# Tile 3's eight chunks in seven half-size products, with weight sums partly on GpSimd

## The chip, the cores and the metric

The kernel runs on one core of one Trainium2 chip. The metric is the device time of one execution in microseconds (us). The core has five engines with instruction streams of their own: TensorE (PE; its weight loads are a row of their own, PEld), VectorE (DVE), ScalarE (ACT), GpSimd (POOL) and SyncE (SP, which here issues nearly all DMAs). Each engine works its stream in order and waits on semaphores for the others.

## The reference, cut to what matters

```python
for b in range(nb):                      # linear attention, decay lam per head, blocks of 64
    intra = einsum('bhic,bhjc->bhij', qb, kb) * Dmask
    intra = einsum('bhij,bhjd->bhid', intra, vb)
    inter = einsum('bhid,bhde->bhie', qb * lam_pow, kv_state)
    out[:, :, sl] = intra + inter
    kv_state = lam_block * kv_state + einsum('bhsd,bhse->bhde', kb * rev_pow, vb)
x = out.transpose(0, 2, 1, 3).reshape(3072, 512)
g = x @ w_gate                           # 512 x 1536
y = ((g / (1 + exp(-g))) * (x @ w_val)) @ w_out
```

Batch 4, 8 heads, 768 positions, head size 64; inputs and output are float32, the products run in bf16.

## The kernel before, in words

The 3072 rows of x are made in 12 attention **groups** of 256 rows (0 to 11); two groups make one **tile** of 512 rows, so there are six tiles, 0 to 5. Of a group g, in this order: `cast_scaled` (L287) casts k on ACT and q (times a decay) on DVE, into a `qk` buffer, and starts the DMA transpose; `v_scale` (L263) makes `v_s`; `upd_mm` (L406) multiplies k and v, ACT copies the result (`ups`, L446); `state` (L468) adds it up on POOL (`kvf`, L479; `kvn`, L459 and L461; `kvs`, L482; `kv`, L483); `scores` (L380) gives a mask product to DVE (L397); `inter`, `intra` (L507, L524) and `evac` (L538) put the group's rows into `xt`. `attend(g)` (L895) does inter of g, `upd_mm` and scores of g+1, intra and evac of g, then `state(g+1)`.

The FFN of a tile has 12 **chunks** fc of 128 hidden columns. A plain chunk (`ffn_fc`, L610) is four matmuls of 128x512 for the gate (L585), SiLU on ACT (L590), four for the value (L603) and a product on DVE (L607) that writes `h`. Chunks 0 to 5 are the first half of the hidden columns, 6 to 11 the second. The tiles 0 to 3 run as plain chunks, the tiles 4 and 5 as three `ffn_unit` calls each (L716). One unit does four chunks (2j, 2j+1, 6+2j, 7+2j) as a 2x2 block product in seven products instead of eight: each is 8 matmuls of 128x256 (L733), for gate and value together. It reads sums of weight blocks (`w_combo`, L681, in `ws`, one of four in place) and sums of x blocks (`x_combo`, L702, in `xs`), both on DVE; ACT copies two of the products (L767, L770), DVE adds (L775, L783) and multiplies (L763), and POOL does one of the four multiplications (L763). The output product is done in the same way from tile 1 on (`out_units`, L805, 84 matmuls a tile), with sums of `h` (`h_combo`, L655, L670, into `hs`) and of w_out (`wo_combo`, L644, L653, into `wt`) on DVE.

The eight PSUM banks go round in a ring (`bank`, L85): a chunk takes two of them, and the PE waits for a bank until ACT or DVE have read what was in it.

The order is written out by hand. `steps` (L1031) lists the chunks, `plan` (L1032) what is issued behind each of them, and the loop at L1184 walks through both. L1107 makes the first four chunks of tile 2 on its first group (`s2h`; the plan of the last of them, `s2`, holds the output of tile 0, attention of group 5 and the sums of `h` and w_out), and L1148 the rest of tile 2 (`sns[2]`: first those four chunks on the second group, then eight full ones) and tile 3 (`sns[3]`). The weight sums are put there by number (L1131): 110 and 112 are in tile 1, 206 and 210 in tile 2, 301 to 309 in tile 3. `trickle` holds the `h` sums, and `drip` issues a few of them behind each step.

```python
    WS = [(x, n, i, 0, 3) for x, n, i in ((110, 0, 0), (112, 0, 1), (206, 1, 0), (210, 1, 1), (301, 2, 0), (303, 2, 1))] + [(308, 3, 0, 0, 2), (309, 3, 1, 0, 2)]
...
        nc.vector.tensor_tensor(out=o, in0=i0, in1=i1, op=op)
```

Here the tuple is place, number of the sum, gate or value, and the columns; the second line is the sum itself (L696), 128x1536 in bf16.

Of the kernel before, what the change touches and what calls it, by code (L numbers as in the profile page):

```python
# [9 lines left out]
BF16 = mybir.dt.bfloat16  # L10
# [27 lines left out]
def _body(ctx, tc, nc, q, k, v, lam, moe_w_gate, moe_w_val, moe_w_out, out):  # L38
# [42 lines left out]
    last_bank = []  # L81

    fixed = []

    def bank():  # L85
# [4 lines left out]
        last_bank.insert(0, ring[0] % 8)  # L90
        b = banks[ring[0] % 8]
        primed[ring[0] % 8] = 0
        ring[0] += 1
        return b

# [186 lines left out]
        for put in held.pop(g, []):  # L282
            put()

    QP = ()

    def cast_scaled(g, eng=nc.vector):  # L287
        eng = nc.gpsimd if g in QP else eng
# [278 lines left out]
    def new_xt(t):  # L567
        st[("xt", t)] = xt_pool.tile([128, 2, MC, 2, BLK], BF16, name="xt", tag="xt")

    HALVED = ((2, 4), (2, 5))  # L570

    def pieces(t, fc, N, b0, b1):
        if (t, fc) in HALVED:
# [104 lines left out]
    ws = {}  # L678
    KH = MC // 2

    def w_combo(i, n, js=(0, 3)):  # L681


        w = (wg_sb, wv_sb)[i]
        if n < 2 and (i, n) not in ws:
            pool, tag = ((v_pool, "v"), (qk_pool, "qk"))[n]
            ws[i, n] = pool.tile([128, KH, FH * 128], BF16, name="ws", tag=tag)
        elif n == 2 and (0, n) not in ws:
            both = h_pool.tile([128, 2, KH, FH * 128], BF16, name="ws", tag="h")
# [10 lines left out]
    XS0 = 4  # L700

    def x_combo(t, n, g):  # L702


        xt = st[("xt", t)]
        g = slice(0, 2) if g is None else slice(g, g + 1)
        b11, b12 = xt[:, g, 0:KH, 0], xt[:, g, 0:KH, 1]
        b21, b22 = xt[:, g, KH:MC, 0], xt[:, g, KH:MC, 1]
        if t not in xs:
            pool, tag = (qkt_pool, "qkt") if t == XS0 else (raw_pool, "raw")  # L710
            xs[t] = pool.tile([128, 3, 2, KH, BLK], BF16, name="xs", tag=tag)
        x = [xs[t][:, m, g] for m in range(3)]
        o, i0, i1 = ((x[0], b12, b11), (x[1], b22, x[0]), (x[2], b21, x[1]), (b12, b22, b12))[n]
        nc.vector.tensor_tensor(out=o, in0=i0, in1=i1, op=ALU.subtract)

    def ffn_unit(t, j, bk, early=None, mid=None, dr=(0, 0, 2)):  # L716


        xt = st[("xt", t)]
# [10 lines left out]
        def product(i, o, lhs, rhs, start=False):  # L730
            for fi in range(2):
                for c in range(KH):
                    nc.tensor.matmul(o[:, fi * 256:fi * 256 + 256], lhs(i, c, 2 * j + fi), rhs(c),  # L733
                                     start=(start and fi == 0 and c == 0), stop=(c == KH - 1),
                                     skip_group_check=True)
# [410 lines left out]
    for t in range(2, 4):
        order = [c for j in range(FC // 4) for c in (2 * j, 2 * j + 1, FH + 2 * j, FH + 2 * j + 1)]
        sn = [step(t, fc, 2 if t == 2 and fc < NH else 0) for fc in (range(FC) if t == 2 else order)]  # L1148
        sns[t] = sn
        if t == 2:  # L1150
            at(sn[4], ahead, 6)
        for j, g in ((4 if t == 2 else 0, 2 * t + 3), (8 if t == 2 else 6, 2 * t + 4)):
            at(sn[j], cast_scaled, g)
            at(sn[j], load_group, g + 1)
            if g > 7:
                at(sn[1 + j], v_scale, g, nc.gpsimd, 0, H // 2)
                at(sn[(1 if t == 2 else 2) + j], v_scale, g, nc.gpsimd, H // 2, H)
        for i in range(2):
            at(sn[AT[t][i]], attend, 2 * t + 2 + i)
        if t == 2:  # L1160
            at(sn[4], out_units, 1, (0,), False, 2)
            at(sn[5], out_rest, 1, (0,), 2, 4)
            at(sn[6], out_rest, 1, (0,), 4, 7)
            at(sn[5], v_scale, 7, nc.vector)
            at(sn[8], out_units, 1, (1,), False, 2)
            at(sn[9], out_rest, 1, (1,), 2, 7)
            at(sn[9], h_combo, t, (0, 2))
        else:
            at(sn[7], h_combo, t, (0, 2))
        at(sn[11], h_combo, t, 2)  # L1170
    sn = sns[3]
    if C11 is not None:
        at(sn[C11], cast_scaled, 11)
# [4 lines left out]
    for x, n, i, j0, j1 in WS:
        at(sns[x // 100][x % 100], w_combo, i, n, (j0, j1))
    if not XM[0]:  # L1180
        for n in (0, 3, 1, 2):
            at(sn[XC], x_combo, 4, n, 0)

    for n, (t, fc, b0, b1) in enumerate(steps):  # L1184
        if t >= 1 and t + 1 < NG // 2 and ("xt", t + 1) not in st:
# [25 lines left out]
    xw = dict(x=x_soon(4, None if XM[0] else 1),
              c=[soon(cast_scaled, 11)] if C11 is None else [],
# [77 lines left out]
```

## Time and profile before

| what | us |
|---|---|
| median of 3 runs (216.4 to 217.43) | 216.51 |
| span of the profiled execution | 214.96 |
| PE busy (97% of the span) | 208.1 |
| DVE busy (69%) | 148.3 |
| ACT busy (61%) | 130.9 |
| POOL busy (43%) | 92.7 |
| granted TensorE clock | full throughout |
| tile 2's first four chunks on its second group | 81.47 to 85 |
| attention 6, attention 7 | from 97.4, from 108.8 |
| tile 3, twelve chunks | 111.7 to 135.4 |
| output of tile 2, 84 matmuls | 135.4 to 144.6 |

The profiled execution's own time outside its span is not recorded; the median lies 1.55 us above the span. Times in the views are counted from the start of the span. A row of the timeline gives start, duration, engine, line, operation, output and inputs, and in brackets how long the engine had stood idle and who ended that. A row of the chain gives start, duration, engine, tile, line and the number of instructions.

### The profile page before, as it was taken

The numbers are of one execution on the slowest core, as the hardware profiler recorded it, in microseconds if no ns is written. First come the engines' busy times: TensorE is split into PE (matmuls) and PEld (weight loads), VectorE is DVE, ScalarE is ACT, GpSimd is POOL, SyncE is SP. The second block draws the span as 40 slices with busy tenths as digits, with TensorE's granted clock in tenths as the row PEclk, the third lists the DMA queues.
The fourth block names the chain that finished last, engine by engine and source line by source line (L and its number), as shares of the span: only waits on it lengthen the run. The fifth ranks groups of instructions, "written<-read, shape, count | busy, mean of one in ns | idle before, by whom it ended". The sixth has DMA issues, their size and how long they took to land.

```text
span 215.0 us, 6856 instructions
## 1 busy us (share of the span) xinstructions
PE 208.1 (97%) x2797; PEld 153.3 (71%) x2801; DVE 148.3 (69%) x267; ACT 130.9 (61%) x280; POOL 92.7 (43%) x128
## 2 busy tenths in 40 slices
PE   8789999999999999999999999999999999999993
PEld 3467445887888548866754545888888888888883
DVE  1773447576677989874569878697988389961940
ACT  5878676756636153638369487774983676636522
POOL 6675755818399440595962153240750022200200
PEclk9999999999999999999999999999999999999999
DMA  6999999999999778899576859855000500005014
GB/s 188 345 354 381 376 336 296 285 226 223 309 387 174 185 212 208 244 214 263 122 198 143 217 121 257 207 121 201 5 3 5 195 0 3 0 0 198 0 52 146
DMA packets 82176, 39.76 MB, mean 185 GB/s; under 512 B 45410, under 2 KB 77794, under 8 KB 82146
## 3 DMA queue, kind: packets, MB, share of 16 engines
q1 hardware_dynamic: 80946, 38.74, 64.7%
q10 hardware_dynamic: 1200, 0.59, 0.9%
q8 instruction: 22, 0.36, 0.7%
q14 instruction: 8, 0.07, 0.1%
HBM read 28.31 MB, written 6.29 MB: 161 GB/s over the span
## 4 chain that ended last, share of the span: by engine, by line
PE 93%; DMA 2%; DVE 1%; SPq 1%; ACT 0%; issue 0%; DVEq 0%
PE bank L823 22%; PE bank L585 20%; PE bank L603 19%; PE bank L733 17%; PE bank L623 5%; PE bank L531 3%; DMA kraw<-in_k_dram 2%; PE bank L518 2%; PE bank L424 2%; PE bank L362 1%; DVE ssb L369 1%; SPq L115 1%; PE bank L392 1%; PE bank L322 1%; ACT qk L306 0%
## 5 line engine op out<-in xcount | busy, mean ns | idle before, releaser
L607 DVE TENSOR_TENSOR h<-sil,bank 128x256 bf16<-128x256 bf16 (+1 forms) x67 | 35.0, 533 | 29.9 <-PE bank L603 17.2
L585 PE MATMUL bank<-xt,wg_sb 128*128 128x256 bf16 (+1 forms) x276 | 52.8, 315 | 0.0
L603 PE MATMUL bank<-xt,wv_sb 128*128 128x256 bf16 (+1 forms) x276 | 52.5, 314 | 0.0
L590 ACT ACTIVATE sil<-bank 128x256 bf16<-128x256 f32 (+1 forms) x67 | 31.6, 481 | 21.8 <-PE bank L585 18.4
L603 PEld LDWEIGHTS <-wv_sb 128*128 128x128 bf16 x276 | 26.9, 98 | 14.8 <-POOL wv_sb L249 0.2
L585 PEld LDWEIGHTS <-wg_sb 128*128 128x128 bf16 x276 | 25.9, 98 | 13.6 <-issue 0.2
L266 POOL TENSOR_TENSOR v_s<-v,dec 128x512 bf16<-128x512 f32 (+1 forms) x18 | 23.0, 1295 | 24.3 <-DMA v<-in_v_dram 17.3
L763 POOL TENSOR_TENSOR h<-sil,es 128x512 bf16<-128x512 bf16 x6 | 7.0, 1165 | 47.4 <-ACT sil L760 47.4
L823 PEld LDWEIGHTS <-h 128*128 128x128 bf16 x240 | 23.3, 98 | 3.4 <-issue 0.3
L823 PE MATMUL bank<-wo_sb,h 128*128 128x256 bf16 x180 | 21.5, 273 | 0.0
L823 PEld LDWEIGHTS <-hs 128*128 128x128 bf16 x180 | 17.6, 98 | 2.7
L369 DVE TENSOR_TENSOR ssb<-bank,causal 128x512 bf16<-128x512 f32 x24 | 15.4, 684 | 1.8 <-PE bank L362 1.8
L479 POOL TENSOR_TENSOR kvf<-kvs,ups 128x256 f32<-128x256 f32 x8 | 6.5, 814 | 20.9 <-ACT ups L446 20.9
L733 PEld LDWEIGHTS <-ws 128*128 128x128 bf16 x144 | 13.8, 98 | 1.8
L823 PE MATMUL bank<-wt,hs 128*128 128x256 bf16 x120 | 15.0, 273 | 0.0
L775 DVE TENSOR_TENSOR bank<-bank,es 128x512 f32<-128x512 f32 x12 | 7.8, 694 | 9.6 <-PE bank L733 9.6
L479 POOL TENSOR_TENSOR kvf<-kvf,ups 128x256 f32<-128x256 f32 x16 | 13.0, 815 | 0.9
L760 ACT ACTIVATE sil<-bank 128x512 bf16<-128x512 f32 x18 | 10.5, 596 | 3.7 <-PE bank L733 3.7
L733 PE MATMUL bank<-xs,ws 128*128 128x256 bf16 x96 | 12.6, 273 | 0.0
L763 DVE TENSOR_TENSOR h<-sil,bank 128x512 bf16<-128x512 bf16 x18 | 11.8, 683 | 0.3 <-ACT sil L760 0.3
L623 PE MATMUL bank<-wo_sb,h 128*128 128x512 bf16 x45 | 10.7, 380 | 0.2
L733 PE MATMUL bank<-xt,wg_sb 128*128 128x256 bf16 x72 | 10.8, 273 | 0.0
(119 smaller groups left out, 360.3 us busy)
## 6 DMA issues: line engine op xcount, KB each, us to landing
out_dram<-osb SPq DMA_DIRECT2D x22, 256.0 KB, 2.6
v<-in_v_dram SPq DMA_DIRECT2D x18, 256.0 KB, 4.6
woraw<-in_moe_w_out_dram SPq DMA_DIRECT2D x6, 512.0 KB, 7.1
kraw<-in_k_dram SPq DMA_DIRECT2D x24, 128.0 KB, 3.4
qraw<-in_q_dram SPq DMA_DIRECT2D x24, 128.0 KB, 3.4
wraw<-in_moe_w_gate_dram SPq DMA_DIRECT2D x5, 512.0 KB, 6.9
wraw<-in_moe_w_val_dram SPq DMA_DIRECT2D x5, 512.0 KB, 7.0
kraw<-in_k_dram SPq DMA_DIRECT2D x4, 512.0 KB, 6.3
```

The costliest lines, as they stand in the source:

```text
L266: eng.tensor_tensor(out=st[("vs", g)][:, h0:h1], in0=st[("v", g)][:, h0:h1].rearrange("p h (s d) -> p h s d", s=2), in1=vfac(g, h0, h1), o ...
L369: nc.vector.tensor_tensor(out=ssb[:, h2, 2 * c:2 * c + 2].rearrange("p a s n -> p a (s n)"), in0=sp[(c, h2)].rearrange("p (a x) -> p a x", ...
L479: nc.gpsimd.tensor_tensor(out=o, in0=f, in1=u, op=ALU.add)
L585: nc.tensor.matmul(gp[:, n0:n1], wg_sb[:, mc, fs], xt[:, g0:g1, mc].rearrange("p g b n -> p g (b n)"), start=(mc == 0 and n0 == 0), stop=( ...
L590: nc.scalar.activation(sil[:, 0:N], gp[:, 0:N], AF.Silu)
L603: nc.tensor.matmul(vp[:, n0:n1], wv_sb[:, mc, fs], xt[:, g0:g1, mc].rearrange("p g b n -> p g (b n)"), start=(mc == 0 and n0 == 0), stop=( ...
L607: nc.vector.tensor_tensor(out=h_sb[:, fc % FH, b0:b1].rearrange("p b n -> p (b n)"), in0=sil[:, 0:N], in1=vp[:, 0:N], op=ALU.mult)
L623: nc.tensor.matmul(ps, st[("h", t, fc // FH)][:, fc % FH, b], wo_sb[:, fc, c0:c1], start=(fc == 0), stop=(fc == FC - 1))
L733: nc.tensor.matmul(o[:, fi * 256:fi * 256 + 256], lhs(i, c, 2 * j + fi), rhs(c), start=(start and fi == 0 and c == 0), stop=(c == KH - 1), ...
L760: nc.scalar.activation(sil[key], src, AF.Silu)
L763: eng.tensor_tensor(out=h_of(half, r), in0=v3(sil[half, r]), in1=v3(src), op=ALU.mult)
L823: nc.tensor.matmul(o, lhs(f), rhs(f), start=(start and f == 0), stop=(f == FH - 1), skip_group_check=True)
```

## The change

Tile 3's chunks 0 to 3 and 6 to 9 become two `ffn_unit` calls; chunks 4, 5, 10 and 11 stay plain, with attention 8 and 9 among them. For that the weight sums are wanted a tile earlier. Of the eight, four move to POOL: sum 0 of the gate behind `s2h`'s second chunk (place 113), sum 0 of the value and sum 1 of the gate behind `s2` (place 200), sum 1 of the value behind the seventh of tile 2's second list (206). The others stay on DVE, behind 206, 207 and 209. Since one sum overwrites w columns of chunks 6 to 9, tile 2 now does its chunks 6 to 11 first and 0 to 5 after them. Tile 3 gets its own x sums, behind attention 7, with a buffer for the fourth. The q cast of group 9 moves from DVE to POOL. The sums of tile 2's `h` all move behind its last chunk, attention 8's evacuation behind chunk 4, and a permutation of the banks fits the ring to the units.

```diff
-    QP = ()
+    QP = (9,)
...
-    HALVED = ((2, 4), (2, 5))
+    HALVED = ((2, 10), (2, 11))
...
-    def w_combo(i, n, js=(0, 3)):
+    def w_combo(i, n, js=(0, 3), eng=None):
...
-        nc.vector.tensor_tensor(out=o, in0=i0, in1=i1, op=op)
+        (eng or nc.vector).tensor_tensor(out=o, in0=i0, in1=i1, op=op)
...
-            pool, tag = (qkt_pool, "qkt") if t == XS0 else (raw_pool, "raw")
-            xs[t] = pool.tile([128, 3, 2, KH, BLK], BF16, name="xs", tag=tag)
+            pool, tag = (qkt_pool, "qkt") if t in XS0 else (raw_pool, "raw")
+            xs[t] = pool.tile([128, 4 if t == 3 else 3, 2, KH, BLK], BF16, name="xs", tag=tag)
...
-            product(i, E[i], wa(0, 1), xb(0, 1), True)
+            product(i, E[i], wa(0, 1), xsum(3) if t == 3 else xb(0, 1), True)
...
+        if add:
+            add()
...
-    s2h = [step(2, fc, 0, 2) for fc in range(NH)]
+    s2h = [step(2, fc, 0, 2) for fc in range(FH, FH + NH)]
...
-    WS = [(x, n, i, 0, 3) for x, n, i in ((110, 0, 0), (112, 0, 1), (206, 1, 0), (210, 1, 1), (301, 2, 0), (303, 2, 1))] + [(308, 3, 0, 0, 2), (309, 3, 1, 0, 2)]
+    PO, DV = nc.gpsimd, nc.vector
+    WS = [(113, 0, 0, 0, 3, PO), (200, 0, 1, 0, 3, PO), (200, 1, 0, 0, 3, PO), (206, 1, 1, 0, 3, PO),
+          (206, 2, 0, 0, 3, DV), (207, 2, 1, 0, 3, DV), (209, 3, 0, 0, 2, DV), (209, 3, 1, 0, 2, DV)]
...
+    sn = [step(2, fc, 2 if n < NH else 0) for n, fc in enumerate([*range(FH, FC), *range(FH)])]
...
+    at(sn[10], attend, 7)
+    at(sn[10], run_later, 1)
+    for n in (0, 3, 1, 2):
+        at(sn[10], x_combo, 3, n, None)
...
+    at(sn[11], h_combo, 2, (0, 2))
+    at(sn[11], h_combo, 2, 2)
...
+    for x, n, i, j0, j1, eng in WS:
+        at(s2 if x == 200 else sns[x // 100][x % 100], w_combo, i, n, (j0, j1), eng)
...
+    def cast9():
+        cast_scaled(9)
+        load_group(10)
+        for c in range(2):
+            v_scale(9, nc.gpsimd, c * H // 2, (c + 1) * H // 2)
+
+    ffn_unit(3, 0, (u0, u1, c0, c1, o0, o1), lambda: kv_flush(0, 2), dr=DU[0], add=cast9, hc=False)
+    ffn_unit(3, 1, (s0, s1, c0, c1, u0, u1), lambda: kv_flush(), dr=DU[1], hc=False)
+    h_combo(3, (0, 2))
+    perm[:] = [o0, o1, s0, s1, c0, c1, u0, u1]
+    ring[0] = 0
+    attend(8, soon=lambda: cast_scaled(10), fns=(None, None))
+    perm[:4] = [s0, s1, o0, o1]
+    load_group(11)
+    drip_2(DP[0])
+    plain(4)
+    evac(8)
...
+    attend(9)
+    run_later(1)
+    plain(FH + 5)
+    h_combo(3, 2)
```

More of the change, by code (lines that the diff above doesn't have):

```diff
@@ L83, in _body @@
     fixed = []
+    perm = list(range(8))
     def bank():
@@ L89, in bank @@
             return banks[fixed.pop(0)]
-        last_bank.insert(0, ring[0] % 8)
-        b = banks[ring[0] % 8]
-        primed[ring[0] % 8] = 0
+        last_bank.insert(0, perm[ring[0] % 8])
+        b = banks[perm[ring[0] % 8]]
+        primed[perm[ring[0] % 8]] = 0
         ring[0] += 1
@@ L631, in take @@
     def take(n, seeded, cols):
-        got = [(ring[0] + i) % 8 for i in range(n)]
+        got = [perm[(ring[0] + i) % 8] for i in range(n)]
         ring[0] += n
@@ L695, in w_combo @@
                          (s[2], a12, s[1], ALU.subtract), (a21, a11, a21, ALU.subtract))[n]
-        nc.vector.tensor_tensor(out=o, in0=i0, in1=i1, op=op)
+        (eng or nc.vector).tensor_tensor(out=o, in0=i0, in1=i1, op=op)
     xs = {}
     SY = 1
-    XS0 = 4
+    XS0 = (3, 4)
     def x_combo(t, n, g):
@@ L709, in x_combo, with ffn_unit @@
         if t not in xs:
-            pool, tag = (qkt_pool, "qkt") if t == XS0 else (raw_pool, "raw")
-            xs[t] = pool.tile([128, 3, 2, KH, BLK], BF16, name="xs", tag=tag)
-        x = [xs[t][:, m, g] for m in range(3)]
-        o, i0, i1 = ((x[0], b12, b11), (x[1], b22, x[0]), (x[2], b21, x[1]), (b12, b22, b12))[n]
+            pool, tag = (qkt_pool, "qkt") if t in XS0 else (raw_pool, "raw")
+            xs[t] = pool.tile([128, 4 if t == 3 else 3, 2, KH, BLK], BF16, name="xs", tag=tag)
+        x = [xs[t][:, m, g] for m in range(4 if t == 3 else 3)]
+        o, i0, i1 = ((x[0], b12, b11), (x[1], b22, x[0]), (x[2], b21, x[1]),
+                     (x[3] if t == 3 else b12, b22, b12))[n]
         nc.vector.tensor_tensor(out=o, in0=i0, in1=i1, op=ALU.subtract)
-    def ffn_unit(t, j, bk, early=None, mid=None, dr=(0, 0, 2)):
+    def ffn_unit(t, j, bk, early=None, mid=None, dr=(0, 0, 2), add=None, hc=True):
         xt = st[("xt", t)]
@@ L798, in ffn_unit @@
         drip(dr[2])
-        h_combo(t, j)
+        if hc:
+            h_combo(t, j)
     def out_row(t, b):
@@ L893, in ahead, with attend @@
         scores(g)
-    def attend(g):
+    def attend(g, back=False, soon=None, fns=(nc.scalar.copy, nc.scalar.copy)):
         run_later(len(later))
         core_a(g)
-        if g + 1 < NG:
-            upd_mm(g + 1)
-            upd_copy(g + 1)
+        upd_mm(g + 1)
+        upd_copy(g + 1)
+        if soon:
+            soon()
+        if not back:
             scores(g + 1)
             late, later[:] = later[:], []
-        core_b(g)
-        if g + 1 < NG:
+        core_b(g, fns)
+        if back:
+            scores(g + 1)
+        else:
             later[:] = late
-            state(g + 1)
+        state(g + 1)
     def set_bank(n):
@@ L1145, in _body, with turn @@
     AT = {2: (7, 10), 3: (A8, A9)}
[L1146 to L1173, printed above, removed]
+    def turn(i, j):
+        x = [(ring[0] + n) % 8 for n in range(i, j)]
+        y = [perm[n] for n in x]
+        for n, b in zip(x, y[1:] + y[:1]):
+            perm[n] = b
+    C8 = 8
+    t = 2
+    sn = [step(2, fc, 2 if n < NH else 0) for n, fc in enumerate([*range(FH, FC), *range(FH)])]
+    sns[2] = sn
+    at(sn[4], ahead, 6)
+    at(sn[4], cast_scaled, 7)
+    at(sn[4], load_group, 8)
+    at(sn[7], attend, 6)
+    at(sn[C8], cast_scaled, 8)
+    at(sn[C8], load_group, 9)
+    for c in range(2):
+        at(sn[9], v_scale, 8, nc.gpsimd, c * H // 2, (c + 1) * H // 2)
+    at(sn[10], attend, 7)
+    at(sn[10], run_later, 1)
+    for n in (0, 3, 1, 2):
+        at(sn[10], x_combo, 3, n, None)
+    at(sn[4], out_units, 1, (0,), False, 2)
+    at(sn[5], out_rest, 1, (0,), 2, 4)
+    at(sn[6], out_rest, 1, (0,), 4, 7)
+    at(sn[5], v_scale, 7, nc.vector)
+    at(sn[8], turn, 1, 4)
+    at(sn[8], out_units, 1, (1,), False, 2)
+    at(sn[9], out_rest, 1, (1,), 2, 7)
+    at(sn[11], h_combo, 2, (0, 2))
+    at(sn[11], h_combo, 2, 2)
     XM = (1, 1)
@@ L1177, in _body @@
     CP = 2
[L1178 to L1182, printed above, removed]
+    for x, n, i, j0, j1, eng in WS:
+        at(s2 if x == 200 else sns[x // 100][x % 100], w_combo, i, n, (j0, j1), eng)
     for n, (t, fc, b0, b1) in enumerate(steps):
@@ L1201, in _body @@
     run_later(len(later))
-    new_xt(5)
-    drip(sum(x[0] == 2 for x in trickle))
     def soon(fn, *a):
@@ L1209, in x_soon, with drip_2, plain @@
         return [soon(x_combo, t, n, g) for n in (0, 3, 1, 2)]
+    def drip_2(n):
+        drip(min(n, sum(x[0] == 2 for x in trickle)))
+    DU = ((0, 0, 1), (0, 0, 0))
+    DP = (2, 0, 2, 2)
+    def plain(fc):
+        ffn_fc(3, fc)
+        kvq_now.append(0)
+        run_later(len(later))
+    hold = trickle[:]
+    trickle[:] = []
+    new_xt(4)
+    p = [perm[(ring[0] + n) % 8] for n in range(8)]
+    (o0, o1, u0, u1, c0, c1, s0, s1) = p
+    trickle[:] = hold
+    def cast9():
+        cast_scaled(9)
+        load_group(10)
+        for c in range(2):
+            v_scale(9, nc.gpsimd, c * H // 2, (c + 1) * H // 2)
[10 more added lines that the diff above has]
+    evac(8)
+    for c in range(2):
+        v_scale(10, nc.gpsimd, c * H // 2, (c + 1) * H // 2)
+    drip_2(DP[1])
+    plain(5)
+    kv_flush(0, 3)
+    drip_2(DP[2])
+    plain(FH + 4)
+    kv_flush()
+    drip_2(DP[3])
+    attend(9)
+    run_later(1)
+    plain(FH + 5)
+    h_combo(3, 2)
+    new_xt(5)
+    drip(sum(x[0] == 2 for x in trickle))
     xw = dict(x=x_soon(4, None if XM[0] else 1),
```

## The prediction

> **What bounds the kernel now.** I read the page's busy shares, then the chain of waits, then the timeline, engine by engine, from 72 to 140 us. The page:
>
> ```profile
> PE 208.1 (97%) x2797; PEld 153.3 (71%) x2801; DVE 148.3 (69%) x267; ACT 130.9 (61%) x280; POOL 92.7 (43%) x128
> PE 93%; DMA 2%; DVE 1%; SPq 1%; ACT 0%; issue 0%; DVEq 0%
> ```
>
> PE is the bound: the chain of waits runs on it for 93% of the span, and from about 38 us on without a break. So PE work that goes is gained in full, and a wait of PE is lost in full; nothing later can win it back. What a unit is worth stands in the chain (start, duration, line, matmuls):
>
> ```profile
> 118.78 0.86 PE bank L585 x4
> 119.64 0.86 PE bank L603 x4
> ...
> 196.28 6.11 PE bank L733 x56
> ```
>
> A plain chunk of tile 3 takes 1.725 us (six of them, 111.88 to 122.23: 10.35 us), a unit 6.11 us (56 matmuls, 109 ns each). The second thing to see is how little slack the engines beside PE have where the new POOL sums go (timeline; DVE above, POOL below):
>
> ```profile
> 78.18 2.27 DVE L670 TENSOR_TENSOR hs<-h 128x768 bf16<-128x768 bf16 x1
> 80.48 0.56 DVE L670 TENSOR_TENSOR h<-h 128x768 bf16<-128x768 bf16 x1
> 80.96 0.55 DVE L670 TENSOR_TENSOR hs<-hs,h 128x768 bf16<-128x768 bf16 x1
> 81.54 0.56 DVE L670 TENSOR_TENSOR hs<-h,hs 128x768 bf16<-128x768 bf16 x1
> 82.02 0.95 DVE L653 TENSOR_TENSOR wt<-wo_sb,wt 128x1536 bf16<-128x1536 bf16 x1
> 82.89 0.95 DVE L653 TENSOR_TENSOR wo_sb<-wo_sb 128x1536 bf16<-128x1536 bf16 x1
> 83.76 0.41 DVE L607 TENSOR_TENSOR h<-sil,bank 128x256 bf16<-128x256 bf16 x1
> ...
> 77.39 2.64 POOL L266 TENSOR_TENSOR v_s<-v,dec 128x1024 bf16<-128x1024 f32 x1 [5.27 <-DMA v<-in_v_dram]
> 88.02 0.72 POOL L479 TENSOR_TENSOR kvf<-kvs,ups 128x256 f32<-128x256 f32 x1 [7.99 <-ACT ups L446]
> ```
>
> The first `hs` took 2.27 us where its equals take 0.55, and it ended 0.42 us after POOL's `v_s` (80.03). So a DVE operation with both inputs in SBUF stands still while POOL runs one, and DVE is in order. The product at 83.76 (L607, inputs `sil` and a PSUM bank) waited in that queue 1.2 us longer than its bank needed.
>
> **The change part by part.** *Matmuls.* Eight plain chunks go (8 x 1.725 = 13.80 us), two units come (2 x 6.11 = 12.22): **-1.6 us**, on the path. The other PE work is the same in amount; the order of tile 2's chunks and the bank permutation cost nothing by themselves.
>
> *Weight sums on POOL, at 80 to 88 us.* POOL's 7.99 us of idleness, above, is where the two of place 200 run: the instruction order puts them behind `v_s` of group 6 and ahead of state 6, and neither waits for anything later than 80 us. How long is one (128x1536, both inputs bf16)? The trace has none on POOL. Below: a one-input cast of 1024 on POOL takes 1.04 us, so 1.5 us. Above: three of L763's POOL products (1165 ns for 512) would take 3.5 us. The nearest in kind is `v_s`, also two inputs: 1.05 us for 512, 2.05 for two, so **3.1 us**. In sentences apart: the Trainium skill, GPSIMD Engine Reference, section 3.1, gives about 2.6 cycles of 1.2 GHz per element for two-input operations, an estimate of 3.3 us, and by it the sum below would be 0.4 us longer.
>
> Each of them holds up DVE's five two-SBUF operations from 80.48 to 83.8. The first `hs` ends at 80.45; POOL's first sum, which has waited since 80.1, takes its turn to 83.5; DVE's next operation ends at 83.9 instead of 81.04 (+2.9); POOL's second sum goes in between and ends at 86.9; the operation after that ends at 87.3 instead of 81.51 (**+5.8**). That they alternate I take from 153 us, where a POOL `kvn` got in between two DVE weight sums that follow each other (0.99 and 0.61 us there instead of 0.42). If DVE kept its turn until 83.8 instead, POOL would hold up the `hs` operations behind it (84.1, 84.9, 85.7), and the products between them, by about as much. So the product that ended at 84.17 ends at 90.0. It frees bank 7, which the value of tile 2's first full chunk wants at 85.84: PE stands for 4.1 us there. The fourth such product (86.16 to 86.57) comes at 92.4, and the first output product, which needs its bank, started at 87.5: PE is then late by **+4.9 us**. Bounds: 0 if POOL's sums held up nothing, for a gain is excluded (nothing in PE's way gets shorter there); 2.0 if only one of them collides (86.57 + 2.9 - 87.5); 5.7 with sums of 3.5 us.
>
> ```profile
> 85.13 0.87 PE bank L585 x8
> 86.00 0.87 PE bank L603 x8
> 86.88 0.38 PE bank L424 x32
> 87.54 1.42 PE bank L823 x12
> ```
>
> These are the rows of the chain that would be torn apart: no gap now. On the mechanism the Trainium skill speaks against this change: SBUF — State Buffer, section "SBUF: two separate sides", calls the port pair that DVE and GpSimd share an exclusive lock, held for a whole instruction, which also a DVE operation with two SBUF inputs needs. The 2.27 us row agrees; a rule by which both merely slow down would give stalls of half the size.
>
> *The sum at place 113* runs after state 5 (ends 72.1) and before `v_s` of group 6 (whose DMA lands at 77.4): a gap of 5.3 us, cost 0. Were it ahead of the `wt` sum at 70.83, that would hold the products for scores 5 (72.3) for up to 2.3 us; with two DVE sums gone from 66 to 70.5, DVE gets there first.
>
> *The sum at place 206 and v_s of group 8.* POOL's row: state 6 (88.02 to 96.84, 8.8 us) starts 4.1 late, at 92.1, and ends at 100.9; the new sum to 104.0; state 7 (98.90 to 106.24, 7.3 us) to 111.4; `v_s` of group 8 (2.05 us) to 113.4. PE needs it for `upd_mm` 8, at 109.06 now and at 114.0 then. It fits, by 0.5 us, without collisions; three DVE sums (0.95, and two of 0.68) now fall into this stretch and can take up to 2.3 us from POOL. Bounds 0 and 1.8; I take a third, **+0.6**. Attention 6 and 7 need `kvn` that come over 3 us ahead now; that cover holds. The DVE sum of place 207 waits for POOL's of 206; behind it on DVE stands one product with several us of slack.
>
> *x sums, casts, copies.* Unit 3,0's second product starts 0.87 us after tile 3's first matmul (111.9) and wants the fourth x sum. Its input, evacuation 7, ends at 111.66; two sums (0.42 each) end at 112.5, but POOL's three `kvf` (110.24 to 113.2) can hold them up by 0.7 each: 0 to 1.1, I take 0.3. ACT gains four copies of 0.6 us per unit and has k's cast (1.04) and three `kvn` copies (1.2) in the first: 7.1 us for 6.1 of PE. The second unit (4.8 us) takes that up, with E's bank perhaps 0.3 late. POOL's q cast 9 (1.9 us by the one of L293 on POOL) comes behind state 8, and frees 1.2 us of DVE; group 9's `v_s` was waiting for its DMA anyway. DMAs keep their order on SP's queue. Evacuation 8 is put behind a chunk that doesn't read it. Together **+0.3**, bounds 0 and 1.4.
>
> Sum: -1.6 + 4.9 + 0.6 + 0.3 = **+4.2 us**, on a span of 214.96: 219.2. The median lies 1.55 us above that span, and I take the same for after: **220.7 us**.
>
> **The rivals.**
> *Faster.* POOL's sums fit into its idle time and hold DVE up no more than its slack (1.7 us at bank 7: 84.17 against 85.84). For it: POOL is idle for just 7.99 us there, and it needs sums under about 1.0 us or no common port. Then state 6 starts at 88.02, and 8.8 + 3.1 + 7.3 + 2.05 put `v_s` 8 at 109.3, 0.3 late: -1.6 + 0.3 + 0.3 = -1.0, 215.5; with every term at 0, 214.9. Against: the 2.27 us row. Chance 0.27.
> *About the same.* Only one sum collides (2.0) and the rest stays in its cover: 216.9; with shorter sums (1.5 us each) DVE is 2.8 late, as much. Chance 0.11.
> *Slower still.* PE comes out of a stall of 4.1 us with a lower speed. At the start of the trace matmuls of 512 take 622 (L188) and 590 ns (L154) where the same take 380 later (L193); a stretch of 3.4 us at half speed costs 1.7: 222.4. No PE gap of that length lies between 38 us and the end, so the trace is silent. The Trainium skill, TensorE: Matmul & The Clock Gate, Part 1, has the clock fall to half after an idle window of some 3.4 us, which is where the length of the stretch could be checked. Chance 0.12.
> The forecast itself (217.7 to 222.0): 0.50.
>
> **How the numbers follow.** Half a per cent, 1.1 us, is about what a measurement of this kernel can tell from no change. Slower by more: 0.50 + 0.12 = 0.62; within: 0.11; faster: 0.27. The range runs from 215.0, which takes in most of the faster case, to 222.8 (the bounds 5.7 and 1.8 with the other terms as taken: 222.7).
>
> **What would show it.** Matmuls: two rows of 56 in the chain, 6.1 us each, in tile 3. Collision: POOL rows of w sums of about 3 us between 80 and 88 us, DVE's L670 and L653 rows there stretched to 3 us, and PE gaps in the value row of tile 2's first full chunk, with DVE's L607 product as releaser. Place 206: a wait of `upd_mm` 8 for POOL. x sums: a wait of the unit's second product for DVE. I am wrong if those DVE rows keep 0.55 and 0.95 us, or if DVE's products come in time all the same.

## The result and the profile after

The changed kernel takes **225.14 us** (median of 4 runs, 224.26 to 225.28) against 216.97 for the kernel before beside it (216.4 to 217.8): a ratio of 1.036, 95% interval 1.0303 to 1.0417. It is slower by about 8 us; the forecast was 4.2, and the time lies above its range. The profiled execution took 225.03 us, with a span of 223.0; the median lies 2.14 us above that span, where the prediction took 1.55.

The page of the changed kernel; busy shares, shares of the chain, and the granted clock in 40 slices:

```profile
PE 210.1 (94%) x2849; PEld 160.0 (72%) x2849; DVE 158.1 (71%) x272; ACT 134.4 (60%) x288; POOL 111.7 (50%) x135
PE 74%; DVE 14%; POOL 6%; ACT 3%; issue 2%; DVEq 0%; POOLq 0%; ACTq 0%
PEclk9999999999999999799999999999999999999999
```

PE's busy time hardly changed (210.1 against 208.1), but the chain left PE for a quarter of the span, where it had held 93% before. The one 7 in the last line says that the clock fell once. Lines of the code stand one to five further down than before (the product L607 is now L608, the h sums L670 are L671); in warm and copies some stand two and four further still, in the kernels from q9_early on seven.

Where PE stood still (the three longest of its waits from 60 to 160 us: line, who ended it, us in all, times, longest; before the change this list is empty):

```profile
PE bank L604 <- DVE h L608: 3.9, 1, 3.9
PE bank L735 <- DVE bank L777: 0.8, 1, 0.8
PE bank L425 <- POOL v_s L267: 0.7, 1, 0.7
```

The first is bank 7, at the value of tile 2's first full chunk. DVE and POOL ahead of it (timelines):

```profile
81.36 3.33 DVE L671 TENSOR_TENSOR h<-h 128x768 bf16<-128x768 bf16 x1
84.61 3.44 DVE L671 TENSOR_TENSOR hs<-hs,h 128x768 bf16<-128x768 bf16 x1
...
90.29 0.41 DVE L608 TENSOR_TENSOR h<-sil,bank 128x256 bf16<-128x256 bf16 x1
```
```profile
80.87 3.40 POOL L697 TENSOR_TENSOR ws<-wv_sb 128x1536 bf16<-128x1536 bf16 x1
84.23 3.40 POOL L697 TENSOR_TENSOR ws<-ws,wg_sb 128x1536 bf16<-128x1536 bf16 x1
```
```profile
90.76 1.03 PE L604 MATMUL bank<-xt,wv_sb 128*128 128x256 bf16 x8 [3.88 <-DVE h L608]
```

Two DVE sums that took 0.56 and 0.55 us now take 3.33 and 3.44, and each ends 0.42 us behind a POOL sum. The trace counts the time that they are held as busy: 5.7 of the 9.8 us that DVE is busier than before are in these two rows. The product that frees the bank ends at 90.7 instead of 84.2; PE starts right behind it.

The starts of the same PE rows in both traces give the account. Each line shows the shift at that row; what is added between two lines was lost, or won, between them.

| PE row | before | after | shift |
|---|---|---|---|
| inter of attention 5 | 72.00 | 72.87 | +0.87 |
| gate of tile 2's first full chunk | 84.97 | 85.84 | +0.87 |
| its value (bank 7) | 85.84 | 90.76 | +4.92 |
| first product of tile 1's output | 87.47 | 93.16 | +5.69 |
| gate of the next chunk | 88.80 | 95.42 | +6.62 |
| attention 6 | 97.40 | 104.02 | +6.62 |
| attention 7 | 108.79 | 115.23 | +6.44 |
| tile 3's first matmul | 111.71 | 119.15 | +7.44 |
| tile 2's output, first product | 135.22 | 143.00 | +7.78 |
| end of the span | 214.96 | 223.0 | +8.0 |

The 0.87 at the head is not from the change, as far as the runs tell: ACT's and POOL's casts of w_out waited for their DMA, and the same row (attention 5) lies anywhere from 71.39 to 73.45 us in the traces of the experiments below, all with the same code up to there or nearly so. A single execution is that uncertain. The four executions of the change lie close together, though (224.26 to 225.28), so how much of the 0.87 a typical one has stays open.

### The profile page after: what moved, and what is told of

It reads as the page before. It is cut to its first block, busy times and chain, and to the rows that moved or that the text cites. A ratio compares the mean times of both kernels' runs of the same rounds, so it can differ in the third digit from the quotient of the medians.

```text
span 223.0 us, 6981 instructions
## 1 busy us (share of the span) xinstructions
PE 210.1 (94%) x2849; PEld 160.0 (72%) x2849; DVE 158.1 (71%) x272; ACT 134.4 (60%) x288; POOL 111.7 (50%) x135
## 4 chain that ended last, share of the span: by engine, by line
PE 74%; DVE 14%; POOL 6%; ACT 3%; issue 2%; DVEq 0%; POOLq 0%; ACTq 0%
PE bank L735 22%; PE bank L828 18%; PE bank L586 11%; PE bank L604 11%; DVE hs L671 4%; DVE h L671 2%; PE bank L624 2%; PE bank L532 2%; POOL kvf L480 2%; PE bank L519 2%; POOL ws L697 1%; DVE h L608 1%; PE bank L363 1%; DVE ssb L370 1%; POOL v_s L267 1%
## 5 line engine op out<-in xcount | busy, mean ns | idle before, releaser
L604 PE MATMUL bank<-xt,wv_sb 128*128 128x256 bf16 (+1 forms) x244 | 44.2, 306 | 3.9 <-DVE h L608 3.9
L608 DVE TENSOR_TENSOR h<-sil,bank 128x256 bf16<-128x256 bf16 (+1 forms) x59 | 29.4, 512 | 25.1 <-PE bank L604 14.8
L586 PE MATMUL bank<-xt,wg_sb 128*128 128x256 bf16 (+1 forms) x244 | 44.3, 306 | 0.5 <-ACT sil L591 0.5
L591 ACT ACTIVATE sil<-bank 128x256 bf16<-128x256 f32 (+1 forms) x59 | 26.7, 466 | 21.2 <-PE bank L586 13.4
L604 PEld LDWEIGHTS <-wv_sb 128*128 128x128 bf16 x244 | 23.8, 98 | 15.0 <-issue 4.1
L586 PEld LDWEIGHTS <-wg_sb 128*128 128x128 bf16 x244 | 22.8, 98 | 10.3 <-issue 0.7
L735 PEld LDWEIGHTS <-ws 128*128 128x128 bf16 x192 | 18.5, 98 | 3.5 <-issue 1.2
L735 PE MATMUL bank<-xs,ws 128*128 128x256 bf16 x128 | 16.9, 272 | 0.8 <-DVE bank L777 0.8
L762 ACT ACTIVATE sil<-bank 128x512 bf16<-128x512 f32 x24 | 13.9, 593 | 3.7 <-PE bank L735 3.7
L765 DVE TENSOR_TENSOR h<-sil,bank 128x512 bf16<-128x512 bf16 x24 | 15.8, 682 | 0.3 <-ACT sil L762 0.3
L735 PEld LDWEIGHTS <-wg_sb 128*128 128x128 bf16 x128 | 12.4, 98 | 2.2 <-issue 0.5
L735 PEld LDWEIGHTS <-wv_sb 128*128 128x128 bf16 x128 | 12.5, 98 | 1.4
```

The costliest lines, as they stand in the source:

```text
L586: nc.tensor.matmul(gp[:, n0:n1], wg_sb[:, mc, fs], xt[:, g0:g1, mc].rearrange("p g b n -> p g (b n)"), start=(mc == 0 and n0 == 0), stop=( ...
L591: nc.scalar.activation(sil[:, 0:N], gp[:, 0:N], AF.Silu)
L604: nc.tensor.matmul(vp[:, n0:n1], wv_sb[:, mc, fs], xt[:, g0:g1, mc].rearrange("p g b n -> p g (b n)"), start=(mc == 0 and n0 == 0), stop=( ...
L608: nc.vector.tensor_tensor(out=h_sb[:, fc % FH, b0:b1].rearrange("p b n -> p (b n)"), in0=sil[:, 0:N], in1=vp[:, 0:N], op=ALU.mult)
L762: nc.scalar.activation(sil[key], src, AF.Silu)
L765: eng.tensor_tensor(out=h_of(half, r), in0=v3(sil[half, r]), in1=v3(src), op=ALU.mult)
```

## The experiments

Three theories were set against each other. **A** is the prediction's: POOL's two sums of place 200 hold DVE's two-SBUF operations, and PE stands at bank 7. **B**: DVE has too much to do (158 us against 148), and where the sums run does not matter. **C**: POOL's queue is what is late. Times are medians; the kernel before took 216.3 to 216.8 beside them.

### The cause alone, taken away and put in

`s200_dve`, only the two sums of place 200 go back to DVE:

```diff
-    (200, 0, 1, 0, 3, PO), (200, 1, 0, 0, 3, PO)
+    (200, 0, 1, 0, 3, DV), (200, 1, 0, 0, 3, DV)
```

> The two weight sums of place 200 run on DVE instead of POOL, in the same place of the order; all else is as after the change (225.1 us). Theory A (the two POOL sums hold DVE's two-SBUF operations, PE stands 4.1 us at bank 7 and runs slowly for a while after it, and POOL's late queue costs 1.0 more at upd_mm 8): these go, -4.2 -1.5 -1.0, and 1.9 us of DVE work before the product at bank 7 cost 0.3 beyond its slack of 1.7: 218.7 us, no PE gap over 0.5 us and no granted clock under 1.0 between 84 and 100 us. Theory B (DVE simply has too much to do there, 158 us against 148, and where the sums run does not matter): DVE gets 1.9 us more, 225 to 227 us. Theory C (POOL's own queue is what is late, state 6 and all behind it, and the DVE rows are a side show): only the 1.0 at upd_mm 8 and a part of the rest come back, 222 to 224 us.

Measured: **219.71 us** (218.78 to 220.46; ratio 1.0123, 1.0059 to 1.0188). The wait at bank 7 and the fall of the clock are gone, although DVE has 1.9 us more to do there. B and C are out for this part. A's number was 1.0 too low. Upd_mm 8 still waits 0.8 us for `v_s`, which A had put down to the late POOL queue, and the first output product still comes 0.9 us later than before, where A had 0.3.

`before_pool`, the other way round: the kernel before, with two of its own DVE sums moved to POOL at place 200, no unit, no x sums:

```diff
-    ..., (206, 1, 0), (210, 1, 1), ...
+    for i in range(2):
+        at(s2, w_combo, i, 1, (0, 3), nc.gpsimd)
```

> The kernel before with one thing changed: its two weight sums of places 206 and 210 run at place 200 on POOL, where the change has its two. No unit in tile 3, no x sums, no cast moved, and the matmuls stand in the same order. Theory A (POOL's sums hold DVE there): +4.8 to the first output product of tile 2, as in the trace after the change, and 0.7 for the lower clock behind the stall, less what two DVE sums taken away later give (nothing on PE's path there): 222.0 us, with one PE gap of 3.9 us in the value row of tile 2's first full chunk. Theory B (DVE's amount of work is what costs): DVE has 1.9 us less to do, so 216.5 us or less. If the cost needs the units or the other edits: under 219.

Measured: **222.38 us** (221.2 to 223.19; ratio 1.0269, 1.0233 to 1.0306). Its longest PE wait:

```profile
PE bank L603 <- DVE h L607: 3.9, 1, 3.9
```

The same wait, to the tenth, with nothing else of the change there. A's number was 222.0. Some 6 us (222.38 against 216.27), three quarters of the loss, need only these two instructions.

### What of a POOL operation holds DVE

`copies` puts two POOL copies from one SBUF input in the place of each sum (these two sums are not computed); `thirds` cuts each sum into three:

```diff
+        if eng is nc.gpsimd and (i, n) in ((1, 0), (0, 1)):
+            for _ in range(2):
+                eng.tensor_copy(out=o, in_=i0)
+            return
```
```diff
-    (200, 0, 1, 0, 3, PO), (200, 1, 0, 0, 3, PO)
+    *[(200, n, i, j, j + 1, PO) for n, i in ((0, 1), (1, 0)) for j in range(3)]
```

> In place of each of the two POOL sums of place 200, POOL makes two copies of 128x1536 from one SBUF input into the same tile (about 1.5 us each, by the one-input cast of 1024 that takes 1.04); these two sums are not computed. POOL is busy about as long in the same place. If any POOL operation on SBUF holds DVE's two-SBUF operations: DVE rows of 2.0 us (0.55 and 1.5) there, PE stands 3 to 4 us at bank 7, 224 to 225 us. If only POOL operations with two SBUF inputs hold them: the DVE rows keep 0.55 and 0.95 us, no wait of PE at bank 7, 219 us. If POOL's late queue were the cost, it stays either way and the time with it, 224 to 225, with DVE's rows short.

> Each of the two POOL sums of place 200 is cut into three of 128x512 (about 1.05 us each); the same work in the same place. If DVE and POOL take turns operation by operation, each holding the other for one whole operation: DVE's five two-SBUF operations from 80.5 us each wait for one third, 5.2 us in all instead of 5.8, with DVE rows of 1.6 and 2.0 us; the stall at bank 7 goes from 4.1 to about 3.4 us and the time to 224.4 us. If DVE gets in whenever it asks: its rows grow by less than 0.5 us each, the stall is gone, 219 us. If POOL holds on through its queue: as with whole sums, 225.1.

Measured: copies 222.34 us, thirds 225.34 (one run each). DVE of copies, then of thirds:

```profile
80.14 1.70 DVE L671 TENSOR_TENSOR h<-h 128x768 bf16<-128x768 bf16 x1
81.77 1.81 DVE L671 TENSOR_TENSOR hs<-hs,h 128x768 bf16<-128x768 bf16 x1
```
```profile
81.93 1.39 DVE L671 TENSOR_TENSOR h<-h 128x768 bf16<-128x768 bf16 x1
83.25 1.51 DVE L671 TENSOR_TENSOR hs<-hs,h 128x768 bf16<-128x768 bf16 x1
```

A copy with one input holds DVE as a sum does: the row is 0.55 plus what is left of the copy. And the two take turns, one operation each: the thirds hold five DVE operations by 0.83 to 0.96 each, the copies four by 1.14 to 1.26, the whole sums two by 2.8 and 2.9 (the change, above). PE's stall (value after gate, less the 0.87 of the gate) is 2.92 us with thirds, 3.20 with copies, 4.05 with whole sums. Cutting the sums up helps little, since more of the pieces find a DVE operation to hold. That thirds takes as long as the change is in part its late head (attention 5 at 73.45, 0.58 behind the change's); the clock, below, falls there too.

### The clock behind the stall

`warm` fills PE's wait with sixteen matmuls on constants:

```diff
+        if (t, fc) == (2, 10):
+            warm_into(banks[perm[ring[0] % 8]], 32)
```

> Sixteen matmuls of 512 columns on constants (3.5 us at full speed) are added between gate and value of tile 2's first full chunk, into the bank that is used next, so that PE works while it would stand; everything else is as after the change. The results are the same. If the slow rows behind the stall (1.5 us in all) are the clock that falls because PE stood: the stall stays 4.1 us long by the starts of its neighbours, the granted clock stays at 1.0 and 1.5 us come back: 223.6 us. If they are slow for another cause (operands, DMA): 225.1. If the stall is shorter than the 3.5 us it has room for: up to 0.5 more than that.

Measured: **224.29 us** (223.32 to 225.28; ratio 1.0334, 1.0273 to 1.0396). The intervals of warm and of the change overlap; the rows are clearer. Warm's PE (the trace has 15 of the sixteen):

```profile
85.23 3.66 PE L194 MATMUL bank<-const-bfloat16-1.0 128*128 128x512 bf16 x15
89.27 1.03 PE L606 MATMUL bank<-xt,wv_sb 128*128 128x256 bf16 x8 [0.38 <-DVE h L610]
```

The value starts 4.92 us behind the gate, as in the change, so the stall is the same; the clock stays full; the gate of the next chunk comes at 93.24, 8.89 behind the first one, against 9.58 in the change and 3.83 before. So the stall alone costs 5.06 by that row, and the clock **0.7**, not the 1.5 that was expected: the first half of the slow stretch lies under DVE's lateness, since DVE's products come late either way.

When does the clock fall? Busy time of PE in stretches of 3.41 us (stretch, its length, PE busy, granted clock, DMA share and GB/s), after the change and in copies:

```profile
84.90:88.32 3.42, 1.98 (x19) 1.00 0.82 209
88.32:91.73 3.41, 0.97 (x10) 1.00 1.06 295
91.73:95.14 3.41, 3.25 (x75) 0.50 0.08 32
```
```profile
84.10:87.50 3.40, 1.57 (x15) 1.00 0.83 212
87.50:90.90 3.40, 1.88 (x72) 1.00 1.02 290
```

The clock is at half for one stretch of 3.41 us exactly, and the stretches lie on a fixed grid: the record of the granted clock in the traces has 85.33, 68.27 and 105.81 us at full speed ahead of it in the change, in early and in best_p (both below), which are 25, 20 and 31 times 3.413. In the change one grid stretch has 2.44 us of idleness, and the next is slow. Copies has a stall of 3.2 us that the grid cuts into 1.8 and 1.5: no fall. Thirds stands for 2.9 us within one stretch (0.76 busy): it falls. The Trainium skill, TensorE: Matmul & The Clock Gate, Part 1, gives such a free-running window of 3413 ns, and half speed after an idle window; the traces agree on the length, but a window here was far from wholly idle, with 0.8 to 1.2 us of matmuls in it (the change, thirds, before_pool), and the measurement decides.

### Place 206, and v_s of group 8

`s206_dve`, only the sum of place 206 goes to DVE:

```diff
-    (206, 1, 1, 0, 3, PO)
+    (206, 1, 1, 0, 3, DV)
```

> Only the weight sum of place 206 goes from POOL to DVE; the two of place 200 stay on POOL. Theory A: the stall at bank 7 and the slow stretch stay, the wait of upd_mm 8 for v_s of group 8 (0.98 us) goes: 224.1 us, up to 224.6 if the 0.95 us on DVE delay a product. Theory B (DVE's amount of work): 225.1 to 226. Theory C (POOL's queue): state 7, v_s 8 and the casts behind come 3.1 us earlier, and 2 to 3 us come back: 222 to 223.

Measured: **224.12 us** (223.14 to 224.83; ratio 1.0323, 1.0269 to 1.0377), the time that A gave, but not for A's reason: upd_mm 8 waits 0.7 us, as after the change. POOL:

```profile
104.70 0.73 POOL L480 TENSOR_TENSOR kvf<-kvs,ups 128x256 f32<-128x256 f32 x1 [2.91 <-ACT ups L447]
```

State 7 waits for `ups` of attention 6 until 104.7 anyway; the POOL sum lay in these 2.9 us and cost next to nothing. By the rows, `v_s` 8 is late because state 7 takes 8.4 us (7.3 before) and `v_s` itself 2.50 (2.05 before): two copies that took 0.85 us together take 1.46, the last copy 0.74 instead of 0.40, each beside a DVE weight sum that stands there now. (An add of 1.70 us instead of 0.72 runs beside DVE's q cast of group 8, which held POOL as long before.) No run takes these DVE sums away, so this cause is read and not tested. Theory C falls here as well. That the median is 1.0 less has no row for it; the head of this execution lies at 72.08, 0.8 ahead of the change's.

`early` puts the first two sums where DVE had them before the change (110 and 112) and the third on POOL at 113; `early_vs` moves `v_s` 8 ahead of state 7 besides:

```diff
-    WS = [(113, 0, 0, 0, 3, PO), (200, 0, 1, 0, 3, PO), (200, 1, 0, 0, 3, PO), ...
+    WS = [(110, 0, 0, 0, 3, DV), (112, 0, 1, 0, 3, DV), (113, 1, 0, 0, 3, PO), ...
...
+    for c in range(2):                                       # early_vs, at sn[9] before
+        at(sn[7], v_scale, 8, nc.gpsimd, c * H // 2, (c + 1) * H // 2)
```

> The first two weight sums run on DVE in the second half of tile 1 (places 110 and 112, where DVE had them before the change), the third on POOL at place 113; place 200 has none; that of 206 stays on POOL. Theory A: besides the 5.7 us of the stall and the slow stretch also the late product at tile 2's first full chunk goes that s200_dve (219.7 us) still had, 1.0 by the starts of the first output product: 218.7 us. What stays is upd_mm 8's wait for v_s 8 (0.8 us) and tile 3's waits (1.1 us). Theory B (DVE's amount of work, wherever it falls): as s200_dve, 219.7, or more.

> As early, and the POOL scaling of v of group 8 runs ahead of state 7 instead of behind it. In s206_dve the wait of upd_mm 8 (0.7 us) stayed although no POOL sum stood ahead of state 7. If v_s 8 is late because state 7 on POOL is held up by DVE's weight sums (its adds of 0.72 us take 1.70): the wait goes, 0.8 less than early: 217.9 us. If state 7, now 2 us later, makes attention 7 wait for its copies: no gain or a loss of up to 1 us.

Measured: early took 219.23 us once, with the clock full, and 223.71, 224.7 and 225.48, with a mean granted clock of 0.985 to 0.992. early_vs took 220.11, 222.45 and 222.66 us with the clock full (0.999 and up), 223.88 and 223.99 at 0.991 and 0.992. Only early's short execution comes near its forecast. early_vs's trace (220.11) has 1.4 us of waiting at attention 7 for state 7's copies and 1.7 for the x sums, and none at place 113. early's trace is of a long execution (223.71). Its DVE, POOL and PE's wait:

```profile
71.21 3.87 DVE L654 TENSOR_TENSOR wt<-wo_sb,wt 128x1536 bf16<-128x1536 bf16 x1
```
```profile
71.18 3.08 POOL L697 TENSOR_TENSOR ws<-ws,wg_sb 128x1536 bf16<-128x1536 bf16 x1
```
```profile
PE bank L363 <- DVE h L608: 2.9, 1, 2.9
```

POOL's sum of place 113 starts 0.03 us ahead of DVE's `wt` sum and holds it for 2.9 us; PE waits 2.9 us at scores 5, and the clock falls. This is the order that the prediction named for place 113 and excluded, and in the change DVE does get there first (`wt` at 71.15, POOL's sum at 71.46). With DVE's two sums back, who is first is a matter of a tenth of a microsecond. early_vs has the same code up to there, and its trace shows the other order:

```profile
70.48 1.03 DVE L654 TENSOR_TENSOR wt<-wo_sb,wt 128x1536 bf16<-128x1536 bf16 x1
```
```profile
71.73 3.09 POOL L697 TENSOR_TENSOR ws<-ws,wg_sb 128x1536 bf16<-128x1536 bf16 x1
```

Here DVE's sum is not held, PE does not wait at scores 5, and the clock stays full. That early's execution of 219.23 us had this order is likely, but not shown.

`best_p` has all four sums on DVE and `v_s` 8 ahead of state 7; `best_d` has the q cast of group 9 on DVE too:

> The changed kernel with all its weight sums on DVE: two at places 110 and 112, one at 200, one at 206, and v of group 8 scaled ahead of state 7, where POOL idled 2.9 us in s206_dve; q of group 9 still cast on POOL. No POOL sum can meet DVE's, so the wait of 2.9 us at the scores of group 5 that early showed in its slow executions goes too. By the starts: tile 2 as before the change, 0.1 later for the sum of place 200; tile 3: -1.6 for the units, +0.4 x sums, +1.0 the adds that wait for POOL's q cast, +0.6 attention 9 and the first product behind it: +0.5 in all, 217.0 us. If the units themselves cost DVE more than it has (theory B): 219 or more.

> As best_p, with q of group 9 cast on DVE (1.23 us) between the two pairs of adds of the first unit. The wait for the first pair (1.0 by the starts) goes; the second pair (L787 in the trace) comes up to 0.85 us later and PE waits for it 0.4: 216.4 us. In q9_dve, disturbed, the second wait was 1.0: then as best_p, 217.0.

Measured: **221.26 us** (220.8 to 222.22; ratio 1.0225, 1.0196 to 1.0254) and 221.6 (1.0193, 1.0148 to 1.0238; the execution with the trace took 738 us, so no row of it is read here). By its number alone best_p is what B gave (219 or more); by its trace, the expectation was wrong on `v_s` 8. POOL of best_p, and PE's wait at attention 7:

```profile
104.22 2.05 POOL L267 TENSOR_TENSOR v_s<-v,dec 128x512 bf16<-128x512 f32 x2 [6.14 <-DMA v<-in_v_dram]
```
```profile
PE bank L519 <- POOL kvn L460: 1.2, 2, 0.9
```

The v of group 8 lands only at 104.2, so POOL stood with state 7 queued behind; its copies came late, PE waited 1.5 us in all, and the clock fell once more.

### What is left without POOL's sums: tile 3

The next kernels keep all four sums on DVE (110, 112, 200, 206) and `v_s` 8 behind state 7. `dve_sums` is just that. `q9_early` casts q of group 9 on DVE between the x sums and the unit's adds. `q9_v8` also scales half of `v_s` 8 on DVE; `v8_late` does so two instructions later; `v8_late_dp` moreover issues two `h` sums of tile 2 behind the masks of attention 9.

```diff
+    WS = [(110, 0, 0, 0, 3, DV), (112, 0, 1, 0, 3, DV), (200, 1, 0, 0, 3, DV), (206, 1, 1, 0, 3, DV), ...
+    at(sn[10], q_scale, 9)                                   # q9_early and on
+    at(sn[9], v_scale, 8, nc.gpsimd, 0, H // 2)              # q9_v8 and on
+    at(sn[9], v_scale, 8, nc.vector, H // 2, H)
+    DP = (0, 2, 2, 2)                                        # v8_late_dp, for (2, 0, 2, 2)
```

> The changed kernel with its four POOL weight sums on DVE (places 110, 112, 200, 206) and nothing else different; v of group 8 is scaled behind state 7 again (in best_p, ahead of it, POOL waited to 104.2 us for v's DMA, state 7 came late and PE stood 1.5 us at attention 7 and ran slowly behind it). This is the change without its part on POOL's weight sums. By the starts against the kernel before: tile 2 +0.1, v_s 8 +0.8, tile 3 +0.5 (-1.6 units, +0.5 x sums, +1.0 the adds behind POOL's q cast, +0.6 attention 9 and behind): 217.9 us. If the units and x sums cost more than the waits seen so far (theory B): 219.5 or more, as s200_dve.

> Only the cast of q for group 9 goes back from POOL (2.16 us, 120.36 to 122.5) to DVE (1.23 us). Theory A: the last two x sums of tile 3 (2.45 us for two, 0.84 alone) are no longer held, the adds into the bank start 1.0 us earlier, and PE's wait for them (0.8 us, 1.0 by the starts) goes: 224.1 to 224.3 us. Theory B: DVE takes 1.2 us more in tile 3 and is the bound there: 225.1 to 226.3.

> As dve_sums, with q of group 9 cast on DVE directly behind the x sums and ahead of the product and the adds of the first unit; k's cast and the transpose stay where they are. In q9_dve the cast ran on DVE behind the first adds, was itself held by POOL's v_s 9 (2.05 us instead of 1.23), and the second adds came 1.0 late. Here POOL has nothing with DVE in the critical 4 us but the adds of state 8: the waits for the first and for the second adds both stay under 0.4: 0.7 less than dve_sums, 217.2 us. If DVE's amount of work is the bound in the unit, no gain.

> As q9_early, and the second half of v of group 8 is scaled on DVE (0.65 us, where DVE idles 1.3 and 2.3 us) instead of POOL, behind state 7 as before. POOL's half ends 1.0 to 1.25 us earlier: the wait of upd_mm 8 (0.8 us) goes, 216.4 us, about the kernel before.

> As q9_v8 (218.05 us), with DVE's half of v of group 8 behind the last adds of tile 1's output instead of ahead of them. In q9_v8 it pushed one of these adds back and PE waited 0.6 for it; here DVE idles 1.3 us at that point. That wait goes, the wait for v_s 8 stays gone: 217.4 us. If v_s 8 is late again at upd_mm 8, as q9_early: 218.7.

> As v8_late, and two of the activation sums (1.2 us each, 1.5 where POOL holds them) that stand on DVE ahead of the masks for attention 9 come two chunks later. In q9_early and q9_v8 PE waited 1.7 and 0.6 us for those masks. If DVE's order in tile 3 is what is left: 0.5 less than v8_late, 216.9 us, the kernel before's time. If DVE's amount of work is the bound there: the sums are late instead, and PE waits as long at the first products of tile 2's output: 217.4.

| kernel | us | ratio, interval |
|---|---|---|
| q9_dve (the change, q cast 9 on DVE) | 224.9 (223.46 to 228.25) | 1.034, 1.0256 to 1.0424 |
| dve_sums | 218.92 | 1.0092, 1.0061 to 1.0122 |
| q9_early | 218.75 | 1.0079, 1.0052 to 1.0107 |
| q9_v8 | 218.05 | 1.0065, 1.004 to 1.0091 |
| v8_late | 217.31 | 1.0041, 1.0017 to 1.0065 |
| v8_late_dp | 218.52 | 1.0102, 1.0067 to 1.0137 |

q9_dve is inconclusive. The change is 8.2 us behind the kernel before beside it, dve_sums 2.1: all POOL's sums cost **about 6 us**. dve_sums, q9_early and q9_v8 came 1.0, 1.5 and 1.6 us above what was expected, v8_late as expected, v8_late_dp 1.1 above the worse of its two numbers. dve_sums still waits, and this is the loss of tile 3. After the change, DVE, POOL and PE at the head of the first unit:

```profile
120.35 2.45 DVE L716 TENSOR_TENSOR xs<-xt,xs 128x512 bf16<-128x512 bf16 x2
```
```profile
120.36 2.16 POOL L294 TENSOR_TENSOR qk<-qraw,qdn 128x1024 bf16<-128x1024 f32 x1 [0.22 <-DMA v<-in_v_dram]
```
```profile
124.06 1.20 PE L735 MATMUL bank<-xs,ws 128*128 128x256 bf16 x8 [0.81 <-DVE bank L777]
```

POOL's q cast holds the last two x sums (0.87 us for two in q9_early, 2.45 here), the adds come late, and PE is 0.97 late by the starts. In q9_early:

```profile
114.53 1.22 DVE L302 TENSOR_TENSOR qk<-qraw,qdn 128x1024 bf16<-128x1024 f32 x1
```
```profile
117.01 1.20 PE L742 MATMUL bank<-xs,ws 128*128 128x256 bf16 x8 [0.36 <-DVE bank L784]
```

Though the cast is now DVE's own, PE's wait falls from 0.8 to 0.36: the mechanism is right. But the median gains only 0.2, within the intervals, since 1.7 us of waiting for masks turn up at attention 9. q9_v8 ends the wait for `v_s` 8 and gets 0.6 of it back in tile 1's output; v8_late ends that too (its trace, of an execution 1.4 us above its median, has 1.1 us at the first unit's adds instead). v8_late_dp then moves only the order and loses 1.2: PE waits 0.7 and 0.4 for products around attention 9 instead. Only this last step lies outside the intervals; from dve_sums to v8_late they still touch. So the late `v_s` 8 and POOL's hold on the x sums are there, each worth 1 us or less, and a wait that is taken away at one place turns up at another, because DVE has hardly any idle time left to take up a delay. In the change, from 132 us on (columns: length, PE, PEld, DVE, ACT, POOL busy, clock, DMA share, GB/s):

```profile
132.00:138.00 6.00, 6.00 (x148) 3.63 (x146) 5.95 (x8) 5.77 (x12) 4.56 (x4) 1.00 0.76 179
138.00:144.00 6.00, 5.76 (x143) 3.38 (x142) 6.00 (x11) 5.10 (x13) 4.61 (x6) 1.00 0.92 242
```

DVE is busy for 11.95 of 12 us there; before the change it was 10.59 in the fullest such stretch of tile 3 (120 to 132 us). But being busy is in part being held again. One `h` sum, after the change and then before it:

```profile
135.35 1.22 DVE L671 TENSOR_TENSOR h<-h 128x1024 bf16<-128x1024 bf16 x1
```
```profile
119.50 0.69 DVE L670 TENSOR_TENSOR h<-h 128x1024 bf16<-128x1024 bf16 x1
```

The six `h` sums from 132 to 144 us take 5.36 us, sums of the same shapes before the change took 3.30. Some 2.1 of the 11.95 us are therefore time in which POOL's state 9, `v_s` 10 and state 10 hold DVE, and DVE's own work, some 9.9 us, is no more than the 10.59 before. v8_late, without any POOL weight sum, is as full (12.00 of 12, 126 to 138 us). No version tried beats the kernel before; the best, 217.31 us, is 0.4% behind it.

## Where the prediction was right, and where it was wrong

By the table of shifts, against the prediction's terms:

- **Matmuls, -1.6: right.** The two units run from 119.15 to 133.05, 13.9 us; less the two waits (0.47 and 0.97) that is 12.5, against 12.22 expected.
- **Weight sums at 80 to 88 us, +4.9: right, in mechanism and size.** The first output product is 5.69 - 0.87 = 4.82 late, the stall at bank 7 4.05 (4.1 expected), the alternation is the one described; POOL's sum takes 3.09 us where it meets nothing (102.58), 3.1 expected. The lock is shown by s200_dve and before_pool. On the page that the prediction weighed, the Trainium skill's SBUF — State Buffer, "SBUF: two separate sides", the runs agree that the hold is exclusive and lasts an instruction, for POOL copies with one input too.
- **Place 113, 0: right, narrowly,** as early and early_vs show.
- **The lower clock: a rival at 0.12, and it came with the forecast.** It is no other way for things to go, but what the forecast's own stall brought, in the change, before_pool, thirds and s206_dve, and did not bring in copies, where the grid cut the stall in two. Its price was 0.7 (warm), not 1.7. It belonged in the sum, which had it at nothing.
- **Place 206, +0.6 with bounds 0 and 1.8: right in size (1.0 from attention 7 to tile 3) and, by the rows, in what it was priced for,** DVE's sums that hold POOL, in state 7 and `v_s` 8. What the prediction let use up the slack, the late state 6 and the POOL sum, cost next to nothing (s206_dve).
- **x sums, casts and copies, +0.3 with bounds 0 and 1.4: this is the step that failed.** Tile 3 is 0.34 longer than before, and 0.29 more go at the first output products, where -1.3 was expected: 1.9 more, so that this term measured 2.2 instead of 0.3. The x sums' first wait was 0.47 (0.3 expected). But POOL's q cast was entered as a relief for DVE ("frees 1.2"), while the lock, priced in full 40 us earlier, was not applied to it: it holds the last two x sums, and PE is 0.97 late by the starts. 0.24 more are in the units, and the other 0.53 come from the end of the units to the first output products, in the 12 us in which DVE is full. dve_sums, 2.1 us slower than the kernel before with no POOL weight sum in it, bears out that tile 3 gives no gain. How the 2.2 divide is read from one trace; q9_early, in which that hold is gone, gained only 0.2 in its median.
- **The head, +0.87,** was in no term; as far as the runs tell, it is the execution's.

The sum: 0.87 of the head, 4.82 of the stall, 0.93 up to the next gate (of it 0.7 the clock), -0.18 before attention 7, 1.0, 0.34 and 0.29 make 8.1 on the span; the median adds 0.6 more (2.14 above the span instead of 1.55). The range missed because its upper end stacked only two terms' bounds, had tile 3 at a gain, and left the clock to a rival of its own.

What stays open: whether tile 3's units gain anything where POOL does not hold DVE from 132 to 144 us (no run moved POOL's state 9 and `v_s` 10 away), and how often early meets the one order at place 113 and how often the other.

## What to carry to other kernels

An idle stretch of POOL is free only if DVE does no operation with two SBUF inputs beside it: count, for each POOL operation that touches SBUF, the DVE operation that it meets, and charge that with nearly POOL's whole duration (2.8 and 2.9 of 3.1 us here), in every place where POOL gets work. A held DVE operation shows as a long busy row and not as idle time, so compare its length with its equals before calling DVE overloaded. A stall of PE costs the stall and, where it filled most of a 3.41 us grid stretch (2.2 to 2.7 us of it in the change, before_pool and thirds), a slow stretch behind it. Where a kernel is bound on one engine for 93% of its chain, the test of a saving on it is whether the engine that feeds it has idle time in the same few microseconds, not over the span.

## What the runs showed of the hardware that was not expected

- The clock fell after grid stretches of 3.41 us in which PE was still busy for 0.76 to 1.23 us (the change, thirds, before_pool, s206_dve, early), and not after those of 1.57 and 1.88 us (copies), 1.72 (before_pool) and 1.98 (the change). In best_p it fell after one with 1.99 us busy (108.66 to 112.07, 77 rows, nearly all of them attention matmuls of 64 columns); so busy time as the trace models it is not all that counts.
- A one-input POOL copy of 128x1536 from bf16 to bf16 takes 1.76 us (two in 3.53, with DVE beside it) and holds DVE like a sum.
